# Linear attention into a gated feed-forward: the numerators of the first batches as pairs of 64-row products

## The chip, the cores and the metric

The kernel runs on one core of a Trainium2 chip. The metric is the device time of one execution in microseconds; a profile of one execution is read beside it. Engines: TensorE (PE, with its weight loads as PEld), VectorE (DVE), ScalarE (ACT), GpSimd (POOL) and SyncE (SP).

## The reference

Inputs q, k, v are 8 batches x 8 heads x 576 positions x 64; the feed-forward weights are 512 x 1536 (gate, value) and 1536 x 512 (out). Everything is float32 outside the kernel.

```python
def phi(x, c, s):
    r = np.maximum(x, 0.0)
    return np.concatenate([r * c, r * s], axis=-1)      # c, s: cos and sin of pi/2 * pos/S
q_p, k_p = phi(q, cos_w, sin_w), phi(k, cos_w, sin_w)
kv  = np.einsum('bhsf,bhsd->bhfd', k_p, v)
z   = np.sum(k_p, axis=2)
num = np.einsum('bhsf,bhfd->bhsd', q_p, kv)
den = np.einsum('bhsf,bhf->bhs', q_p, z)[..., None] + 1e-06
x   = (num / den), heads side by side                    # 4608 tokens x 512
g   = x @ w_gate
out = (g * (1.0 / (1.0 + np.exp(-g))) * (x @ w_val)) @ w_out
```

## The kernel before

**Tiles and groups.** A token tile `t` holds 128 tokens: two slots `c` of 64 positions. A batch has `NC` = 9 slots, so tile 4 holds the last slot of batch 0 and the first of batch 1. Four tiles make a token group `tg`, which goes through the feed-forward; nine groups. Groups 1 and up use a Strassen-like scheme for the products (`block_jobs`, L977, and `out_jobs`, L1142) beside plain ones (L904, L1052, L1262).

**Heads.** The 8 heads are numbered 2g + e, with e = 0 or 1 and g = 0 to 3; g is split again as 2j + i. Heads with i = 0 have their 64 features on SBUF rows 0 to 63, heads with i = 1 on rows 64 to 127.

**The attention numerators.** `kvd` (batch 0) and `kvd1` (batch 1) hold, for each e, j and w (w = 0 for cosine, 1 for sine), a block-diagonal matrix: the kv of the head i = 0 in the upper 64 rows and first 65 columns, the kv of the head i = 1 in the lower 64 rows and last 65 columns, zeros elsewhere. The 65th column of a head is z, so a product gives 64 numerators and the denominator. A product with 128 rows and 130 columns does two heads at once; the two w accumulate in PSUM. A tile takes 8 such products, and two PSUM banks hold its result. Batches 2 to 7 are done otherwise (L785: one head per product, cosine and sine on 128 rows, 65 columns) and aren't touched.

- Tiles 0 to 3, in a start phase written out by hand in `words`: `a_tile` (L372) makes the products, in two halves j = 0 and 1; `x_den` (L388), `x_rec` (L397) and `x_mul` (L401) divide, on VectorE; `x_turn_pe` (L418) turns x with the identity on TensorE; `x_turned` (L323) copies it to `xT`. For tile 0 the halves are separate down to the copies, and half j has PSUM bank j to itself; for tiles 1 to 3 bank e holds the heads of that e. `z` words put idle products (L187) between. `turn_q` (L351) turns the queries in between and `weight_q` (L360) makes the sine-weighted ones.
- Tiles 4 to 8: `tile_jobs` (L779 for batches 0 and 1) with the same block-diagonal products; tile 4's go in halves of 64 tokens, by batch. The denominators are on ScalarE (L797), reciprocal and multiplication on VectorE (L803, L807). Tiles 4 to 7 are turned on TensorE (L755); tile 8, like all later ones, by a transposing DMA (L747). `turned_tiles` (L1310, L1326) makes their queries.

**The order.** The words of the start phase are issued in the order written. The middle of them reads:

```
kvo10@dve a0.0 kvo11@act qr1@dve z1 den0.0 qw1.1
a0.1 den0.1 tq3 rec0.0 rec0.1 tq2 a1.0 a1.1 z2 x0.0 qr3@act x0.1 den1 xt0.1 qw3.1 xt0.0 rec1 qr2@act
xc0.1@act qw2.1 a3.0 x1.0 a3.1 a2.0 den3 xc0.0@act a2.1 G1.0 xt1.0
```

Everything later is a list of jobs with costs, due times and rooms (banks, buffers), which a planner in the kernel (`order_once`) puts into one order per engine while the program is built. The waits themselves come from the framework, which orders accesses to the same memory. The planner's costs for the touched jobs aren't changed, nor the number of jobs or their rooms.

## Time and profile before

| what | value |
|---|---|
| time, median of 3 runs | 298.6 us (298.52 to 299.35) |
| span of the profiled execution, first to last instruction | 296.4 us |
| mean granted TensorE clock | 0.998 |
| TensorE busy | 291.1 us, 98% |
| VectorE busy | 252.0 us, 85% |
| ScalarE busy | 199.4 us, 67% |

The profile is of one execution, for which only its span is given; the timed runs include what lies around the span, so the median stands 2.2 us above it. A line such as L779 is the line of the kernel that issued the instruction. Lengths of matmuls overlap, since they are pipelined: what one costs is read from start to start. A shape like 128\*64 128x130 is the weights (rows\*columns) and the moving operand (rows x columns).

### The profile page before, as it was taken

What the parts mean: (1) busy time and instruction counts of PE and PEld (TensorE: products, weight loads), DVE (VectorE), ACT (ScalarE), POOL (GpSimd) and SP (SyncE); (2) the same over time, 40 slices, a digit from 0 to 9 for tenths busy, and PEclk for the clock granted to TensorE, in tenths of its full rate; (3) what the DMA queues carried; (4) which work ended last, traced back from release to release, by engine and by line L of the source; (5) the groups of instructions that cost most, each with busy time, mean ns of one, the idle gap of its engine ahead of it and who ended that gap; (6) DMA issues with size and microseconds to landing.
All of it is one profiled execution on the core that took longest, in us unless ns stands there. A gap on an engine that the chain in (4) does not pass through costs nothing.

```text
span 296.4 us, 8073 instructions
## 1 busy us (share of the span) xinstructions
PE 291.1 (98%) x3244; PEld 238.7 (81%) x3244; DVE 252.0 (85%) x514; ACT 199.4 (67%) x421; POOL 69.6 (23%) x122
## 2 busy tenths in 40 slices
PE   8999999999999999999999999999999999999994
PEld 4597465776787888898898889888988888888883
DVE  7878997879877999999988987998679868986883
ACT  6564346989559968985699589967465556565630
POOL 7963630003007012221352023200220050002000
PEclk9999999999999999999999999999999999999999
DMA  7999999997989997799996979940470046002026
GB/s 266 225 196 198 202 206 207 203 205 121 194 177 144 229 190 122 151 171 149 174 203 133 186 113 162 183 81 2 107 110 2 0 97 119 2 0 73 0 58 157
DMA packets 71973, 40.89 MB, mean 138 GB/s; under 512 B 48768, under 2 KB 68736, under 8 KB 71936
## 3 DMA queue, kind: packets, MB, share of 16 engines
q0 software_dynamic: 24800, 24.39, 49.1%
q1 hardware_dynamic: 46528, 15.47, 28.9%
q10 hardware_dynamic: 608, 0.52, 0.7%
q8 instruction: 25, 0.41, 0.6%
q14 instruction: 12, 0.10, 0.1%
HBM read 37.75 MB, written 9.44 MB: 159 GB/s over the span
## 4 chain that ended last, share of the span: by engine, by line
PE 97%; DVE 1%; issue 0%
PE banks L977 45%; PE banks L1142 24%; PE banks L1052 5%; PE banks L1262 4%; PE banks L438 4%; PE banks L904 4%; PE banks L187 3%; PE banks L716 3%; PE banks L785 2%; PE banks L779 1%; PE banks L372 1%; PE banks L1310 0%; PE banks L315 0%; PE banks L418 0%; PE banks L351 0%
## 5 line engine op out<-in xcount | busy, mean ns | idle before, releaser
L1111 POOL DMA_DIRECT2D out_dram<-ob x52 | 27.3, 532 | 104.8 <-ACT ob L630 69.7
L1036 ACT ACTIVATE sg<-banks 128x512 bf16<-128x512 f32 x72 | 41.3, 599 | 5.6 <-PE banks L977 5.4
L977 PEld LDWEIGHTS <-wg_sb 128*128 128x128 f16 x384 | 36.9, 98 | 6.3
L628 ACT COPY banks<-banks 128x512 f32<-128x512 f32 (+1 forms) x53 | 29.9, 572 | 17.5 <-PE banks L977 7.3
L1142 PEld LDWEIGHTS <-ht 128*128 128x128 f16 x384 | 37.4, 98 | 4.8
L1072 DVE TENSOR_TENSOR ht<-sg,banks 128x512 f16<-128x512 bf16 x60 | 39.9, 680 | 0.9 <-PE banks L977 0.6
L977 PEld LDWEIGHTS <-wgs_sb 128*128 128x128 f16 x368 | 35.7, 98 | 4.6
L997 DVE TENSOR_TENSOR banks<-m,banks 128x512 f32<-128x512 f32 x44 | 30.2, 693 | 10.6 <-ACT m L628 8.1
L977 PEld LDWEIGHTS <-wv_sb 128*128 128x128 f16 x320 | 31.0, 98 | 3.8
L977 PE MATMUL banks<-kvt,wgs_sb 128*128 128x256 f16 x236 | 33.4, 273 | 0.0
L1142 PEld LDWEIGHTS <-sums 128*128 128x128 f16 x288 | 27.9, 98 | 3.3
L630 ACT ACTIVATE ob<-banks 128x512 f32<-128x512 f32 x32 | 18.8, 596 | 15.9 <-PE banks L1142 15.2
L977 PE MATMUL banks<-xT,wg_sb 128*128 128x256 f16 x192 | 28.8, 273 | 0.0
L628 ACT COPY m<-banks 128x512 f32<-128x512 f32 x44 | 25.5, 590 | 4.4 <-PE banks L977 4.3
L1142 PE MATMUL banks<-wo_sb,ht 128*128 128x256 f16 x192 | 25.7, 273 | 0.0
L1142 PE MATMUL banks<-wt_sb,sums 128*128 128x256 f16 x192 | 24.9, 273 | 0.0
L977 PE MATMUL banks<-xT,wv_sb 128*128 128x256 f16 x160 | 24.0, 273 | 0.0
L1036 ACT ACTIVATE sg<-m 128x512 bf16<-128x512 f32 x24 | 15.1, 630 | 12.4 <-DVE m L1005 12.2
L807 DVE TENSOR_TENSOR x<-banks,rec 128x512 f16<-128x512 f32 x32 | 21.6, 686 | 1.5 <-DVE rec L803 0.2
L977 PE MATMUL banks<-kvt,wg_sb 128*128 128x256 f16 x168 | 22.4, 273 | 0.0
L1142 PE MATMUL banks<-wt_sb,ht 128*128 128x256 f16 x192 | 22.3, 273 | 0.0
L877 ACT ACTIVATE r_q<-raw_q,tanq 128x256 bf16<-128x256 bf16 x45 | 20.7, 510 | 0.1
(160 smaller groups left out, 544.7 us busy)
## 6 DMA issues: line engine op xcount, KB each, us to landing
out_dram<-ob POOLq DMA_DIRECT2D x52, 128.0 KB, 3.9
raw_kv<-in_k_dram POOLq DMA_DIRECT2D x7, 576.0 KB, 5.9
raw_q<-in_q_dram POOLq DMA_DIRECT2D x12, 288.0 KB, 10.7
raw_kv<-in_v_dram POOLq DMA_DIRECT2D x6, 576.0 KB, 8.3
out_dram<-ob SPq DMA_DIRECT2D x12, 128.0 KB, 2.5
wg_sb<-in_moe_w_gate_dram POOLq DMA_DIRECT2D x5, 256.0 KB, 8.9
wv_sb<-in_moe_w_val_dram POOLq DMA_DIRECT2D x5, 256.0 KB, 9.5
wo_sb<-in_v_dram SPq DMA_DIRECT2D x2, 576.0 KB, 4.2
```

The costliest lines, as they stand in the source:

```text
L438: nc.tensor.matmul(out=st["f", tg, fc, lo][i], lhsT=(wg_sb, wv_sb)[i][:, kc, fs], rhs=xT[tg][:, ts, kc], start=(kc == 0), stop=(kc == KC - 1))
L628: nc.scalar.copy(out=out, in_=in_)
L630: nc.scalar.mul(out=out, in_=in_, mul=mul)
L807: tt(out=one(x_all, x).rearrange("p (y e d) -> p e y d", e=2, d=D), in0=view()[:, :, :, 0:D], in1=rec_all[:, t % 4].rearrange("p (e y) o - ...
L877: nc.scalar.activation(out=home()[:, :, c, 1], in_=raws[b, "q"][:, :, c], func=AF.Relu, scale=tanq[:, c:c + 1])
L977: nc.tensor.matmul(out=to[:, i], lhsT=a[:, c, 2 * u + i], rhs=x()[:, :, c], start=first and i == 0 and c == 0, stop=c == KH - 1, skip_grou ...
L997: tt(out=bank(c), in0=one(m7_all, m).rearrange("p i x -> p (i x)"), in1=bank(b), op=ALU.add)
L1036: nc.scalar.activation(out=gates(rooms[w])[:, :, jh * HT:(jh + 1) * HT], in_=src, func=AF.Silu, scale=DOWN)
L1052: nc.tensor.matmul(out=bank(v), lhsT=wv_sb[:, kc, fc * P:(fc + 1) * P], rhs=xT[tg][:, :, kc], start=(kc == 0), stop=(kc == KC - 1))
L1072: tt(out=ht[:, 4 * u + w:4 * u + w + 3:2, jh * HT:(jh + 1) * HT], in0=gates(rooms[w])[:, :, jh * HT:(jh + 1) * HT], in1=src.rearrange("p ( ...
L1111: {"POOL": nc.gpsimd, "SP": nc.sync, "ACT": nc.scalar}[j.eng].dma_start(out=out_v[idx // NC, idx % NC][:, cols], in_=ob_of(t)[e * SH:(e + ...
L1142: nc.tensor.matmul(out=to, lhsT=a[:, kc, i * P:(i + 1) * P], rhs=b[:, kc], start=first and kc == 0 and i == 0, stop=kc == HC - 1, skip_gro ...
```

## The change

Each product of 128 rows and 130 columns becomes two of 64 rows and 65 columns: one per head, on that head's rows only, without the zeros. The head i = 0 writes one PSUM bank, the head i = 1 the other, and the two are issued one after the other. So a tile takes 16 products instead of 8, with 16 weight loads; tile 4, in halves of 64 tokens, 32 instead of 16. This is so for tiles 0 to 8; tile 0 loses its separate banks for the halves. The result `x` then has its 128-column blocks in another order, which the turns on TensorE undo (`by_pairs`). Tile 8 is turned by a DMA, which can't, so its multiplication is split in two, one per j, that write the old order.

```diff
+    def by_pairs(kc):
+        return kc % 2 * J + kc // 2
+    def halves_of(i):
+        return slice(i * D, (i + 1) * D)
...
     def a_tile(t, j):
...
         for e in range(2):
             for w in range(2):
-                nc.tensor.matmul(
-                    out=(ps[:, j, 2 * e * D1:2 * (e + 1) * D1] if t == 0 else
-                         ps[:, e, 2 * j * D1:2 * (j + 1) * D1]),
-                    lhsT=(qwT[t % 2] if w else qr[t])[:, e, j].rearrange("p c s -> p (c s)"),
-                    rhs=kvd[:, e, j, w].rearrange("p i x -> p (i x)"),
-                    start=(w == 0), stop=(w == 1),
-                )
+                for i in range(2):
+                    rows = halves_of(i)
+                    nc.tensor.matmul(
+                        out=ps[:, i, (2 * j + e) * D1:(2 * j + e + 1) * D1],
+                        lhsT=(qwT[t % 2] if w else qr[t])[rows, e, j].rearrange("p c s -> p (c s)"),
+                        rhs=kvd[rows, e, j, w, i], start=(w == 0), stop=(w == 1))
...
     def x_den(t, ps, ys=slice(0, 4)):
...
-            in0=a_view(t, ps, ys)[:, :, :, D:D1],
+            out=heads(st["den", t])[:, :, ys], in0=by_rows(ps)[:, :, ys, D:D1],
...
     def x_turn_pe(t, ks=slice(0, KC)):
...
-            nc.tensor.transpose(out=ps[:, kc], in_=st["x", t][:, kc * P:(kc + 1) * P], identity=ident16)
+            nc.tensor.transpose(out=ps[:, kc], in_=st["x", t][:, by_pairs(kc) * P:(by_pairs(kc) + 1) * P], identity=ident16)
...
     def tile_jobs(t, key, by_pe=False):
...
                         if b < 2:
-                            if g % 2:
-                                continue
                             for w in range(2):
-                                nc.tensor.matmul(
-                                    out=ps[ms, e, g * D1:(g + 2) * D1],
-                                    lhsT=late[:, 2 * (t % 2) + w, e, g // 2].rearrange("p c s -> p (c s)")[:, ms],
-                                    rhs=(kvd1 if b else kvd)[:, e, g // 2, w].rearrange("p i x -> p (i x)"),
-                                    start=w == 0, stop=w == 1)
+                                for i in range(0 if g % 2 else 2):
+                                    rows = halves_of(i)
+                                    nc.tensor.matmul(
+                                        out=ps[ms, i, (g + e) * D1:(g + e + 1) * D1],
+                                        lhsT=late[rows, 2 * (t % 2) + w, e, g // 2].rearrange("p c s -> p (c s)")[:, ms],
+                                        rhs=(kvd1 if b else kvd)[rows, e, g // 2, w, i], start=w == 0, stop=w == 1)
                             continue
...
         def fn(j):
-            tt(out=one(x_all, x).rearrange("p (y e d) -> p e y d", e=2, d=D), in0=view()[:, :, :, 0:D],
-               in1=rec_all[:, t % 4].rearrange("p (e y) o -> p e y o", e=2).to_broadcast([P, 2, 4, D]), op=ALU.mult)
+            x_, rec_ = one(x_all, x), heads(rec_all[:, t % 4])
+            if pairs and not by_pe:
+                for jj in range(J):
+                    ys = slice(2 * jj, 2 * jj + 2)
+                    tt(out=x_.rearrange("p (j i e d) -> p j i e d", i=2, e=2, d=D)[:, jj], in0=view()[:, :, ys, 0:D],
+                       in1=rec_[:, :, ys].to_broadcast([P, 2, 2, D]), op=ALU.mult)
+                return
...
```

More of the change, by code (lines that the diff above doesn't have):

```diff
@@ L371, in a_tile, with by_rows, heads @@
             for w in range(2):
-                nc.tensor.matmul(
-                    out=(ps[:, j, 2 * e * D1:2 * (e + 1) * D1] if t == 0 else
-                         ps[:, e, 2 * j * D1:2 * (j + 1) * D1]),
-                    lhsT=(qwT[t % 2] if w else qr[t])[:, e, j].rearrange("p c s -> p (c s)"),
-                    rhs=kvd[:, e, j, w].rearrange("p i x -> p (i x)"),
-                    start=(w == 0), stop=(w == 1),
-                )
-    def a_view(t, ps, ys):
-        if t == 0:
-            return ps[:, ys.start // 2, 0:4 * D1].rearrange("p (e y x) -> p e y x", e=2, x=D1)
-        return ps[:, :, 0:2 * J * D1].rearrange("p e (y x) -> p e y x", x=D1)[:, :, ys]
+                for i in range(2):
[4 more added lines that the diff above has]
+                        rhs=kvd[rows, e, j, w, i], start=(w == 0), stop=(w == 1))
+    def by_rows(ps):
+        return ps[:, :, 0:2 * J * D1].rearrange("p i (y x) -> p i y x", x=D1)
+    def heads(ap):
+        return ap.rearrange("p (i y) o -> p i y o", i=2)
     def x_den(t, ps, ys=slice(0, 4)):
@@ L388, in x_den @@
         nc.vector.tensor_scalar(
-            out=st["den", t].rearrange("p (e y) o -> p e y o", e=2)[:, :, ys],
-            in0=a_view(t, ps, ys)[:, :, :, D:D1],
+            out=heads(st["den", t])[:, :, ys], in0=by_rows(ps)[:, :, ys, D:D1],
             scalar1=eps_all[:, 2 * t:2 * t + 1], scalar2=DOWN, op0=ALU.add, op1=ALU.mult)
@@ L396, in x_rec @@
             st["x", t] = x_all[:, t % NX]
-        nc.vector.reciprocal(out=st["rec", t].rearrange("p (e y) o -> p e y o", e=2)[:, :, ys],
-                             in_=st["den", t].rearrange("p (e y) o -> p e y o", e=2)[:, :, ys])
+        nc.vector.reciprocal(out=heads(st["rec", t])[:, :, ys], in_=heads(st["den", t])[:, :, ys])
     def x_mul(t, ps, ys=slice(0, 4)):
         nc.vector.tensor_tensor(
-            out=st["x", t].rearrange("p (y e d) -> p e y d", e=2, d=D)[:, :, ys],
-            in0=a_view(t, ps, ys)[:, :, :, 0:D],
-            in1=st["rec", t].rearrange("p (e y) o -> p e y o", e=2)[:, :, ys].to_broadcast(
-                [P, 2, ys.stop - ys.start, D]), op=ALU.mult)
+            out=st["x", t].rearrange("p (i y d) -> p i y d", i=2, d=D)[:, :, ys], in0=by_rows(ps)[:, :, ys, 0:D],
+            in1=heads(st["rec", t])[:, :, ys].to_broadcast([P, 2, ys.stop - ys.start, D]), op=ALU.mult)
     xT = {}
@@ L754, in fn @@
             for kc in range(KC):
-                nc.tensor.transpose(out=ps[:, kc], in_=one(x_all, x)[:, kc * P:(kc + 1) * P], identity=ident16)
+                nc.tensor.transpose(out=ps[:, kc], in_=one(x_all, x)[:, by_pairs(kc) * P:(by_pairs(kc) + 1) * P], identity=ident16)
         mm = pe(230, fn, key, after=after, get=[r], put=[x])
@@ L791, in view @@
         def view():
-            return bank(r)[:, :, 0:2 * J * D1].rearrange("p e (y x) -> p e y x", x=D1)
+            return by_rows(bank(r))
+        pairs = bs[-1] < 2
         def fn(j):
-            o, i_ = den_all[:, t % 4].rearrange("p (e y) o -> p e y o", e=2), view()[:, :, :, D:D1]
+            o, i_ = heads(den_all[:, t % 4]), view()[:, :, :, D:D1]
             if j.eng == "ACT":
@@ L806, in fn @@
         def fn(j):
-            tt(out=one(x_all, x).rearrange("p (y e d) -> p e y d", e=2, d=D), in0=view()[:, :, :, 0:D],
-               in1=rec_all[:, t % 4].rearrange("p (e y) o -> p e y o", e=2).to_broadcast([P, 2, 4, D]), op=ALU.mult)
+            x_, rec_ = one(x_all, x), heads(rec_all[:, t % 4])
[5 more added lines that the diff above has]
+                return
+            tt(out=x_.rearrange("p (i y d) -> p i y d" if pairs else "p (y e d) -> p e y d", d=D, **({"i": 2} if pairs else {"e": 2})),
+               in0=view()[:, :, :, 0:D], in1=rec_.to_broadcast([P, 2, 4, D]), op=ALU.mult)
         mul = Job({"DVE": d1(512)}, fn, after=[rec], get=[x], put=[r, one_at])
```

## The prediction

> **What bounds the kernel now.** I read the page first, then the busy time by stretches, then the timeline of TensorE (PE) where the change sits.

> ```profile
> span 296.4 us, 8073 instructions
> PE 291.1 (98%) x3244; PEld 238.7 (81%) x3244; DVE 252.0 (85%) x514; ACT 199.4 (67%) x421; POOL 69.6 (23%) x122
> PE 97%; DVE 1%; issue 0%
> ...
> 12.00:18.40 6.40, 6.39 (x107) 5.45 (x107) 5.65 (x20) 3.58 (x9) 5.15 (x7) 1.00 1.58 189
> ...
> 57.00:292.00 235.00, 234.87 (x2619) 203.15 (x2618) 203.40 (x386) 166.41 (x351) 42.51 (x78) 1.00 0.68 119
> ```

> The third line is the chain of work that ended last: 97% PE. The last two lines are the stretches (window, its length, then PE, PEld, DVE, ACT and POOL busy, granted clock, DMA). From 57 to 292 us PE is busy 234.87 of 235.00 us at full clock. So a nanosecond taken off PE's issue before that counts at the end, unless some input of PE is then late. Busy time isn't issue time, though; what PE's issue costs must be read from starts.

> ```profile
> 45.10 0.63 PE L779 MATMUL banks<-phit 128*128 128x130 bf16 x8
> 45.57 0.39 PE L755 MATMUL banks<-ident,x 128*128 128x128 f16 x4
> 45.79 0.63 PE L779 MATMUL banks<-phit 128*128 128x130 bf16 x8
> 46.26 0.59 PE L1262 MATMUL banks<-wo_sb,ht 128*128 128x512 f16 x2
> ...
> 65.81 0.42 PE L785 MATMUL banks<-kv,phit 128*128 128x65 bf16 x8
> 66.07 0.60 PE L977 MATMUL banks<-xT,wgs_sb 128*128 128x256 f16 x4
> ...
> 206.28 0.60 PE L977 MATMUL banks<-xT,wv_sb 128*128 128x256 f16 x4
> 206.81 0.46 PE L785 MATMUL banks<-kv,phit 128*64 128x65 bf16 x16
> 207.20 0.61 PE L1142 MATMUL banks<-wt_sb,ht 128*128 128x256 f16 x4
> ...
> L977 PE MATMUL banks<-xT,wg_sb 128*128 128x256 f16 x192 | 28.8, 273 | 0.0
> ```

> All but the last line are PE's timeline: start, length, line, tiles, weights, moving operand, count. The last is a group of the page; one product of 256 columns is 273 ns long. Three prices come from them:
> - An old product, 128 rows by 130 columns: (45.57 - 45.10)/8 = 0.059 us. One tile of eight takes 0.47 us.
> - A product of 65 columns on the whole array: (66.07 - 65.81)/8 = 0.0325 us, weight load included.
> - A tile of 16 products of 65 columns on half the array each (here halves by column), two at a time. Before it, four products of 256 columns at (0.60 - 0.27)/3 = 0.11 us would end their slots at 206.72; the half-array work starts at 206.81, so the **change of array shape costs 0.09 us** going in. From its start to the next shape's first product is 0.39 us: eight pairs at 0.0325 = 0.26, and 0.13 for coming out. In and out together: 0.48 us.

> Nothing in the trace of before does what the change does, half the rows with all 128 columns in pairs. The nearest on both counts:

> ```profile
> 38.37 1.24 PE L716 MATMUL banks<-phit,raw_kv 64*64 64x130 bf16 x72
> 39.59 0.38 PE L1262 MATMUL banks<-wo_sb,ht 128*128 128x512 f16 x1
> ...
> 8.03 0.22 PE L242 MATMUL banks<-wt_sb 64*128 64x128 f16 x1
> 8.18 0.61 PE L187 MATMUL banks<-zeros 128*128 128x512 bf16 x2
> ...
> 7.80 0.09 PEld L240 LDWEIGHTS <-wt_sb 64*128 64x128 f16 x1 [0.42 <-issue]
> 7.82 0.10 PEld L242 LDWEIGHTS <-wt_sb 64*128 64x128 f16 x1
> ```

> L716 runs 64x64 quarters: 72 products in 39.59 - 38.37 - 0.09 = 1.13 us are 0.016 each, a quarter of 0.059. So halves by row do run side by side, when they write different banks, as both there and in the change. L242 is a 64x128 product of 128 columns; its slot is 0.055 (four transposes of 128 columns fill 45.57 to 45.79), yet the next full-array product starts 0.15 later. So the 64x128 shape pays 0.09 too. The two weight loads of that shape start 0.02 apart, so two per pair fit into 0.0325 or nearly (0.03 to 0.04). I take 0.0325 per pair; upper end 0.065, if the two take turns; a lower end below 0.0325 has no row.

> [...]

> **The change, part by part.**

> *Tiles 4 and 5* (L779, now 64-row products).

> ```profile
> 41.41 0.24 PE L779 MATMUL banks<-kvt,phit 128*64 128x130 bf16 x1
> 41.41 0.24 PE L779 MATMUL banks<-phit 128*64 128x130 bf16 x1
> 41.49 0.22 PE L779 MATMUL banks<-kvt,phit 128*64 128x130 bf16 x1
> ...
> 41.84 0.80 PE L779 MATMUL banks<-phit 128*64 128x130 bf16 x9
> 42.57 0.64 PE L1310 MATMUL banks<-ident,raw_q 128*64 128x128 bf16 x16
> ```

> Tile 4 spans both batches, so its products already go by halves of the columns, in pairs (41.41 twice). From its first product to L1310, the next shape, the two tiles take 42.57 - 41.41 = 1.16 us, with three shape changes: in, between them, out. After the change there are three as well (128x128, 64x64, 64x128, 128x64). Tile 4 becomes 32 products in four streams of eight, tile 5 sixteen in two streams of eight: 0.26 + 0.13 each, 0.78 us together. **-0.38 us.** Ends: if rows don't overlap, 2 x (0.52 + 0.13) = 1.30, +0.14.

> *Tiles 6, 7, 8* stand alone between 128x128 work (45.10 to 45.57, 45.79 to 46.26; tile 8 likewise). Each goes from 0.47 to 0.09 + 0.39 = 0.48: what the pairs save, two new shape changes take. **+0.03 us** for the three.

> *Tile 8's multiplication* becomes two of half the size.

> ```profile
> 55.95 0.68 DVE L807 TENSOR_TENSOR x<-banks,rec 128x512 f16<-128x512 f32 x1
> ...
> 13.50 0.74 DVE L401 TENSOR_TENSOR x<-banks,rec 128x256 f16<-128x256 f32 x2
> ```

> Two halves take 0.74, one whole 0.68: +0.06 us on VectorE (DVE), which is 0.06 us for the sum that follows it there. Its result goes to a transposing DMA, for a token group that PE comes to later. I price it at 0, at most 0.06.

> *Tiles 0 to 3* (L372), the start.

> ```profile
> 12.24 0.41 PE L372 MATMUL banks<-kvt,wt_sb 128*128 128x130 bf16 x4
> 12.48 0.38 PE L187 MATMUL banks<-zeros 128*128 128x512 bf16 x1
> 12.70 0.39 PE L372 MATMUL banks<-kvt,wt_sb 128*128 128x130 bf16 x4
> 13.02 0.64 PE L351 MATMUL banks<-ident,raw_q 128*64 128x128 bf16 x16
> 13.59 0.64 PE L372 MATMUL banks<-kvt,wt_sb 128*128 128x130 bf16 x8
> ...
> 17.05 0.40 PE L418 MATMUL banks<-ident,x 128*128 128x128 f16 x4
> ...
> 12.69 0.22 DVE L388 TENSOR_SCALAR den<-banks,eps 128x4 f32<-128x4 f32 x1
> 13.15 0.22 DVE L388 TENSOR_SCALAR den<-banks,eps 128x4 f32<-128x4 f32 x1
> 14.34 0.23 DVE L388 TENSOR_SCALAR den<-banks,eps 128x8 f32<-128x8 f32 x1
> 14.48 0.41 DVE L360 TENSOR_TENSOR wt_sb<-wt_sb,tanT 128x512 bf16<-128x512 bf16 x1
> 16.30 0.69 DVE L401 TENSOR_TENSOR x<-banks,rec 128x512 f16<-128x512 f32 x1
> ...
> 14.95 1.04 PE banks L372 x15
> ```

> Here a wait is added. Tile 0's halves had a bank each; now both halves write both banks. The second half (PE, 12.70) comes in the program after the first half's denominators (DVE, 12.69 to 12.91), which read those banks. If accesses are ordered by bank, it waits for them; if by columns, it does not, and the price is nil. I take the wait. PE picks up 0.06 after DVE lets go (L360 ends at 14.89, the chain has PE's L372 at 14.95): start 12.97 in place of 12.70. Queued behind it on PE are L351's transposes, for which ScalarE's relu waits, and tile 1. Four pairs 0.13 and 0.13 out: L351 at 13.23, +0.21; tile 1 likewise at 13.80. On DVE the second denominators wait too: last pair at 13.07, some 0.2 for its result (L785's length, 0.42 less seven steps) and 0.06 to pick up, so 13.33, +0.18. DVE then runs on to 14.24 (13.50 + 0.74), where before it paused: the next denominators start at 14.34, 0.10 after that end, though a DVE row that waits for nothing starts some 0.09 before the previous one ends (14.48 against 14.34 + 0.23 = 14.57). That slack, 0.19, takes up the 0.18. These denominators need tile 1, whose results come at 13.80 + 7 x 0.0325 + 0.2 = 14.23, as before (13.59 + 0.64). From there DVE is where it was.

> PE gets to tiles 3 and 2 later (two new shape changes), does them in 16 pairs, 0.52 instead of 16 x 0.059 = 0.94, and comes to the first gate products some 0.1 early. It can't use it: the turn at 17.05 waits for DVE's 16.30 + 0.69 = 16.99, plus 0.06. **0 us** for the start; ends: -0.1, and +0.2 if DVE's slack isn't there.

> [...]

> **Sum:** -0.38 + 0.03 + 0 + 0 = -0.35 us. The profiled span goes from 296.4 to about 296.05. The median of the runs is 298.6, 2.2 above the span; I leave those 2.2 alone: **298.2 us**.

> **The rivals.**
> - *The rows take turns* (slower). Then a pair costs 0.065. For: a product of 64 rows still loads 128 columns of weights, so there are twice the loads, and no row shows two such loads side by side in different rows. Against: L716's quarters, and loads 0.02 apart. Price: tiles 6 to 8 (0.09 + 0.52 + 0.13 - 0.47) x 3 = +0.81; tiles 4 and 5 +0.14; at the start tile 0's second half lasts to 13.36, tile 1 begins 0.34 late and takes 0.26 us longer, its result comes at 13.93 + 0.49 + 0.2 = 14.62, the denominators at 14.68, +0.34 for DVE and so for 17.05. Together +1.3: **299.9 us**. It decides from 0.041 per pair: there 40 pair slots (8 in each of five tiles) eat what was gained. [...]
> - *The shape isn't charged* (faster). If a 64x128 product between 128x128 ones drains nothing, tiles 6 to 8 take 0.26 each, -0.63, and 4 and 5 lose one or two charges, -0.2: **297.4 us**. L242's 0.15 speaks against it.
> - *The gain is given back* (no change). PE, 0.35 us early from 42 us on, meets an input that isn't early, or DVE's slack at 14.3 fails. For: PE never waits now, so the trace doesn't tell by how much its inputs lead. Against: inputs of that stretch come from PE's own results by way of ScalarE and DVE, and move with it. **298.6 us.**

> **How the numbers follow.** Forecast 0.48, its own range 297.7 to 298.5; given back 0.18 (298.4 to 298.9); turns 0.24; not charged 0.10. About 0.3%, 0.9 us, is what a measurement of this kernel can tell from no change: below 297.7 is faster, above 299.5 slower. Faster: 0.10, and 0.03 from the forecast's edge: 0.13. Slower: 0.24 and 0.01 of the given back: 0.25. The rest, 0.62, is the same. The range leaves out the uncharged case and what is above the turns: 297.6 to 299.9.

> **What would show it.** Right: a timeline of tiles 6 to 8 with 16 products in about 0.48 us including both changes; tiles 4 and 5 in 0.78 up to L1310; tile 0's second half at 12.97; the turn still at 17.05; the last PE work 0.35 us sooner. Wrong: pairs starting 0.05 or more apart (turns); no 0.09 on either side (not charged); PE gaps after 42 us that are no shape change (given back); the turn at 17.2 or later (slack not there).

## The result: slower, and by more from run to run

The changed kernel takes 300.8 us (median of 20 runs, 297.88 to 306.71), the kernel before 298.93 (20 runs, 298.36 to 299.35); the ratio is 1.0053, 95% interval 1.003 to 1.0075. Here and below, medians, ranges and counts are of all runs, while the ratios leave out runs more than 1.5% above the fastest of their kernel: 3 of 20 here, 4 of 12 for the tiles-only kernel and for the kernel before with 96 more rows, 3 of 12 for the late one, and one each for the changed kernel with 144 more rows and the kernel before with 160. The forecast was 298.2. The profiled execution is the fastest of the twenty, 297.88 us: one page can't show what the other nineteen lost, so it is read for the mechanism, and the spread of the runs for the size. The page, the stretches and the timeline of PE, after the change:

```profile
span 296.1 us, 8234 instructions
PE 290.0 (98%) x3324; PEld 237.2 (80%) x3324; DVE 252.1 (85%) x515; ACT 199.3 (67%) x421; POOL 69.3 (23%) x122
PE 95%; DVE 2%; DMA 1%; issue 1%
```

```profile
12.00:18.40 6.40, 5.69 (x133) 4.74 (x132) 5.48 (x20) 3.27 (x8) 5.17 (x8) 1.00 1.59 191
57.00:292.00 235.00, 234.76 (x2619) 203.15 (x2616) 203.42 (x386) 166.03 (x350) 42.09 (x78) 1.00 0.68 119
```

```profile
12.19 0.39 PE L187 MATMUL banks<-zeros 128*128 128x512 bf16 x1
12.68 0.30 PE L380 MATMUL banks<-kvt,wt_sb 64*128 64x65 bf16 x8
12.91 0.58 PE L351 MATMUL banks<-ident,raw_q 128*64 128x128 bf16 x14
...
14.59 0.43 PE L380 MATMUL banks<-kvt,wt_sb 64*128 64x65 bf16 x16
15.63 0.42 PE L380 MATMUL banks<-kvt,wt_sb 64*128 64x65 bf16 x16 [0.61 <-issue]
...
41.46 0.22 PE L782 MATMUL banks<-kvt,phit 64*64 64x65 bf16 x2
42.19 0.25 PE L1321 MATMUL banks<-ident,raw_q 128*64 128x128 bf16 x2
...
45.23 0.40 PE L758 MATMUL banks<-ident,x 128*128 128x128 f16 x4
45.56 0.42 PE L782 MATMUL banks<-phit 64*128 64x65 bf16 x16
45.91 0.60 PE L1273 MATMUL banks<-wo_sb,ht 128*128 128x512 f16 x2
```

From 41 us on the forecast is seen: tiles 4 and 5 take 42.19 - 41.46 = 0.73 us. At the start something is new: PE was busy 6.39 of 6.40 us from 12 to 18.4, now 5.69. In front of tile 2's products it stands 0.61 us "<-issue": no semaphore, no data. The view of all that PE waited for puts it shortest; the first row of each kernel is the wait for the first zeros, which all have:

```profile
PE banks L187 <- DVE zeros L182: 1.0, 1, 1.0
PE banks L380 <- issue: 0.6, 1, 0.6
```

The kernel before has the first of these rows and nothing else. The experiments start from the second.

### The profile page after: what moved, and what is told of

It is laid out like the page before. It is cut to its first block, busy times and chain, and to the rows that moved or that the text cites. A ratio compares the mean times of both kernels' runs of the same rounds, so it can differ in the third digit from the quotient of the medians.

```text
span 296.1 us, 8234 instructions
## 1 busy us (share of the span) xinstructions
PE 290.0 (98%) x3324; PEld 237.2 (80%) x3324; DVE 252.1 (85%) x515; ACT 199.3 (67%) x421; POOL 69.3 (23%) x122
## 4 chain that ended last, share of the span: by engine, by line
PE 95%; DVE 2%; DMA 1%; issue 1%
PE banks L988 46%; PE banks L1153 25%; PE banks L1063 5%; PE banks L1273 4%; PE banks L441 4%; PE banks L915 4%; PE banks L719 3%; PE banks L787 3%; DMA wo_sb<-in_v_dram 1%; DVE v L293 1%; PE banks L782 1%; PE banks L1321 0%; PE banks L380 0%; PE banks L315 0%; PE banks L758 0%
## 5 line engine op out<-in xcount | busy, mean ns | idle before, releaser
L988 PE MATMUL banks<-xT,wg_sb 128*128 128x256 f16 x192 | 28.8, 273 | 0.0
L1047 ACT ACTIVATE sg<-m 128x512 bf16<-128x512 f32 x24 | 15.1, 630 | 12.4 <-DVE m L1016 12.2
L818 DVE TENSOR_TENSOR x<-banks,rec 128x512 f16<-128x512 f32 x31 | 21.0, 688 | 1.3
## 6 DMA issues: line engine op xcount, KB each, us to landing
raw_q<-in_q_dram POOLq DMA_DIRECT2D x12, 288.0 KB, 10.9
```

Of the source, the lines that this page charges most:

```text
L818: tt(out=x_.rearrange("p (i y d) -> p i y d" if pairs else "p (y e d) -> p e y d", d=D, **({"i": 2} if pairs else {"e": 2})), in0=view()[: ...
L988: nc.tensor.matmul(out=to[:, i], lhsT=a[:, c, 2 * u + i], rhs=x()[:, :, c], start=first and i == 0 and c == 0, stop=c == KH - 1, skip_grou ...
L1047: nc.scalar.activation(out=gates(rooms[w])[:, :, jh * HT:(jh + 1) * HT], in_=src, func=AF.Silu, scale=DOWN)
```

## The experiments

Every run was timed beside the kernel before, whose median was 298.68 to 298.93 each time.

**The changed kernel again, each half alone.** `e1_again` is unchanged; `e2_start_only` keeps the pairs of tiles 0 to 3 (`a_tile` and its divisions) with the old `tile_jobs`; `e3_tiles_only` the other way round.

> The changed kernel, unchanged, for its spread and a profile of an execution that isn't its fastest. Known: 297.9 to 306.7 us over 20 executions, the profiled one 297.9 with a span of 296.1, before 298.4 to 299.4. Theory A (the start): in a longer execution the extra microseconds stand as PE gaps between 12 and 38 us, where products wait for VectorE or for weights from DMA; the rest is as in the short one. Theory B (the pairs of tiles 4 to 8): the extra stands at or behind 41 us. Theory C (PE's instruction stream): the extra stands as gaps in which PE waits for no engine and no DMA of the program. Under each the median is 299.5 to 302.

> Only tiles 0 to 3 go by pairs; tiles 4 to 8 are as before. Theory A: spread and median as the changed kernel's (median 300 to 301, some executions above 302). Theory B: as before, 298.4 to 299.4. Theory C (instructions): 64 of the 160 added instructions are in it, so the spread may be less, but is not gone.

> Only tiles 4 to 8 go by pairs; tiles 0 to 3 are as before. Theory A: the spread is that of before (within 1 us) and the median is the forecast gain, 0.35 below before: 298.5. Theory B: spread and median as the changed kernel's. Theory C: 96 of the 160 added instructions, some spread.

| kernel | median, us | lowest to highest (12 runs) | ratio, 95% |
|---|---|---|---|
| again | 300.95 | 299.04 to 303.24 | 1.0073 (1.004 to 1.0105) |
| start only | 299.15 | 298.58 to 300.15 | 1.0007 (0.9984 to 1.003) |
| tiles only | 299.76 | 297.45 to 306.32 | 0.9978 (0.9936 to 1.0019) |

What PE waited for beside the zeros, again, start only and tiles only in turn:

```profile
PE banks L380 <- issue: 1.1, 1, 1.1
PE banks L988 <- DMA xT<-x: 0.5, 1, 0.5
```

```profile
PE banks L380 <- issue: 0.8, 1, 0.8
```

```profile
PE banks L998 <- DMA xT<-x: 1.6, 1, 1.6
```

By the ratios neither half alone is shown to be slower than the kernel before (both intervals hold 1); the whole is. There are two kinds of loss in the traces: the issue wait, in the changed kernel, its repeat and the start-only kernel, and waits for a transposing DMA (`xT`), at 74.8 us in one run and 144.3 in another.

The issue wait always stands at the same place of PE's stream. Counting PE's weight loads and products in order, each as one row, from 0, the row behind the gap is number 447 in all three. What ends it shows in the DMA view, in stretches of 1 us that begin with a packet of the instruction queue, at 13.29 us in the changed kernel and at 14.70 in the repeat:

```profile
q8 instruction: 1, 0.02, 6.1%
```

```profile
q8 instruction: 1, 0.02, 5.9%
```

and the end of the gap in the repeat in its timeline:

```profile
15.43 0.44 PE L380 MATMUL banks<-kvt,wt_sb 64*128 64x65 bf16 x16
16.97 0.42 PE L380 MATMUL banks<-kvt,wt_sb 64*128 64x65 bf16 x16 [1.10 <-issue]
```

A packet of 0.02 MB (16 KB) takes 5.9% of 16 engine-us, 0.95 us. PE goes on at 15.63 and 16.97, 1.3 to 1.4 us behind the packet's end each time. I read it as PE having run out of instructions. The kernel before has such a packet from 13.75 to 14.70 too, so by the same 1.35 us its instructions were usable by about 16.05 (an estimate); its row 447 is a feed-forward product (L438), reached only at 16.72. The pairs at the start bring 48 more rows ahead of that point and run through them faster, and row 447 is tile 2's first product, due at 14.86.

If rows come in blocks of 256, an instruction added anywhere moves every later boundary to another product. So the next kernels move boundaries without touching the attention, or touch it without moving them, by the number of idle products of zeros at the very start:

```diff
-    idle_products(12)
-    idle_products(40, 16)
-    idle_products(4)
+    idle_products(8)            # e4: 96 more rows in about the same time
+    idle_products(94, 16)
+    idle_products(2)
```

**The kernel before with 96 more rows, tiles only with 80 fewer, and two others.** In `e5_tiles_rows` the three calls are (8), (4), (4). `e6_tiles_hold` is the tiles-only kernel with two holds on POOL that read tile 9 and tile 19 (`xT[2][0:1, 1, ...]`, `xT[4][0:1, 3, ...]`) where they read tile 8 and batch 5's features. `e7_tiles_late` issues two products of zeros, 512 columns, ahead of tile 5's. The first kernel has 94 small products, as in the diff; the 98 in its expectation is a slip, for 94 give the 96 rows.

> The kernel before with its attention untouched; only the idle products of zeros at the very start are 98 small and 10 large ones where they were 40 small and 16 large, so that every later instruction of PE stands 96 rows further on in its stream, as the pairs put it, at the same start-up time. Theory F (PE ran out of fetched instructions in front of tile 2's products): PE's stream comes in pieces of 256 rows, and the piece that begins near its row 447 is late. That row is then the turning of q for tile 3 or the products of tile 0 or 1 (L351, L372, at about 13.1 us), and PE stands there 0.7 to 2 us with no semaphore to wait for; the median goes up by 0.3 to 1.5, to 299.2 to 300.4. If the spread of the changed kernel (297.9 to 306.7) also comes from where later pieces begin, the spread of this kernel is like that of the tiles-only kernel (297.5 to 306.3). Theory R (the pairs themselves, or the time at which PE comes to a product, make the waits): no gap at row 447, 298.9 as before, highest run under 300.

> Tiles 4 to 8 by pairs, tiles 0 to 3 as before, and 40 fewer idle products at the start, so that from tile 8 on the rows of PE stand within 16 of where the kernel before has them. Theory F for the spread (later pieces of the instruction stream begin at bad places): the spread goes, highest run under 300, median 298.3 to 298.6 (the 0.38 gained at tiles 4 and 5). Theory R (PE comes 0.38 us earlier to the transposes and races the bulk loads): the spread stays as in the tiles-only kernel, a third of the runs over 300, median 299 to 300.

> Tiles 4 to 8 by pairs, tiles 0 to 3 as before, and two holds of the bulk loads on POOL read another tile: batch 3's loads wait until tile 9's transpose has landed, not tile 8's, and batch 6's until tile 19's has, not the features' of batch 5. Nothing else moves. Theory R (tile 9's or tile 19's transposes are issued 0.1 to 1.7 us ahead of 2 to 4 bulk loads and, when the lead is small, land 6 to 7 us after their issue instead of 2.4 to 4): the stalls of PE at 74.8 us (0.71 in the repeat of the changed kernel) and at 144.3 us (1.77 in the tiles-only kernel) cannot occur; the highest run comes down under 301, the median to 298.3 to 298.6. Theory F: nothing changes, median 299.8, runs up to 306.

> Tiles 4 to 8 by pairs, tiles 0 to 3 as before, and two idle products of 512 columns in front of tile 5's products, 0.43 us, which gives back the 0.38 us that the pairs of tiles 4 and 5 gained. If PE's coming earlier is what makes the later waits for transposes (R): spread as before the change, median 298.8 to 299.1, highest under 301. If it is the pairs' rows in the stream (F) or tile 8's split division: the spread stays, median near 300, runs up to 306.

| kernel | median, us | lowest to highest | ratio, 95% |
|---|---|---|---|
| before, +96 rows | 300.98 | 298.34 to 305.31 (12) | 1.0042 (1.0015 to 1.007) |
| tiles only, -80 rows | 298.49 | 298.02 to 298.81 (12) | 0.9989 (0.9976 to 1.0002) |
| tiles only, holds | 305.09 | 303.17 to 306.81 (6) | 1.0201 (1.0161 to 1.0241) |
| tiles only, late | 301.29 | 298.93 to 307.01 (12) | 1.0052 (1.0026 to 1.0078) |

The first two speak for the rows. The attention of the kernel before, with nothing but more idle rows ahead of it, is as slow and as uneven as the changed kernel; the pairs of tiles 4 to 8 with the rows taken out elsewhere are even, in the narrowest spread of all. The first isn't purely that: in its profile, whose span is 2.8 us longer, 0.2 stands in the idle products, 0.7 is a wait for raw queries at the start, and 1.7 comes behind tile 5. PE's coming earlier doesn't look like the reason: the last kernel, with 0.43 us given back, is slower still. PE's waits in the first and the last:

```profile
PE banks L977 <- DMA xT<-x: 1.4, 1, 1.4
PE banks L187 <- DVE zeros L182: 1.0, 1, 1.0
PE banks L351 <- DMA raw_q<-in_q_dram: 0.7, 1, 0.7
```

```profile
PE banks L1002 <- DMA xT<-x: 1.6, 1, 1.6
```

The second has an issue wait of its own, in the middle of tile 5's products; its timeline, and the instruction packet in a stretch from 40.66 us:

```profile
41.93 0.48 PE L792 MATMUL banks<-phit 64*64 64x65 bf16 x13
42.88 0.26 PE L792 MATMUL banks<-phit 64*128 64x65 bf16 x5 [0.47 <-issue]
```

```profile
q8 instruction: 1, 0.02, 5.9%
```

The row behind this gap is number 958, a weight load: 511 rows behind 447, and between the two stands one semaphore instruction of PE (at 39.43 us), so 512 instructions, two blocks of 256. The packet ends at 41.61, 1.27 ahead of 42.88. The block before begins with row 703, which runs at 38.37 here; the 256 rows in between, among them 72 quarter products at 0.016 us each and tile 4's pairs, are through by 42.2. Its packet begins 40.66 - 38.37 = 2.3 us behind that row, and in the changed kernel the one of row 447 begins 13.29 - 10.37 = 2.9 us behind row 191. So a block seems to be asked for when the one before it begins. In the four profiles with a gap of 0.47 us or more it was usable 4.5 to 5.8 us after that (42.87 - 38.37 here; row 191 at 10.37 and row 447 at 15.63 in the changed kernel). It also says why the gap that I expected in the first kernel didn't come: there row 191 is an idle product, at 7.28 us, the packet began at 10.79, and row 447 ran at 14.4.

The holds (third kernel) were a failure: the two transposes landed 2.4 and 4.7 us after their issue, without a wait of PE, but batch 3's loads started 2.4 us later than in the tiles-only kernel and landed 4.0 to 4.6 later. PE then waited 3.6 us for a bank that ScalarE empties (L641). ScalarE itself stood 4.2 us ahead of that copy, until a DMA that turns features (`phit<-r_q`) had landed, at 91.63 us where it took until 86.61 in the tiles-only kernel. The wait, ScalarE's row, and the stretches around it (PEclk is the number behind POOL):

```profile
PE banks L729 <- ACT m L641: 3.6, 1, 3.6
```

```profile
91.73 0.91 ACT L898 ACTIVATE r_q<-raw_q,tanq 128x256 bf16<-128x256 bf16 x2 [4.20 <-DMA phit<-r_q]
```

```profile
89.40:93.10 3.70, 0.14 (x2) 0.10 (x1) 0.84 (x2) 1.37 (x4) 0.62 (x2) 1.00 0.03 8
93.20:95.10 1.90, 1.90 (x73) 1.71 (x73) 0.94 (x2) 1.90 (x5) 1.90 (x4) 0.59 0.39 25
95.10:97.00 1.90, 1.90 (x10) 1.32 (x9) 0.34 (x1) 1.47 (x4) 1.16 (x3) 0.51 1.15 193
97.00:99.00 2.00, 2.00 (x30) 1.69 (x29) 1.00 (x3) 1.30 (x5) 0.25 (x1) 1.00 1.21 207
```

This run tells nothing on the spread.

**The whole change, the tiles, and the kernel before, at chosen rows.** The idle calls are (8), (118, 16), (2); (12), (16, 16), (4); and (7), (127, 16), (2).

> The changed kernel whole, with 118 small and 10 large idle products at the start where it has 40 small and 16 large: 144 more rows ahead of the work, in about the same time. Theory F: PE's rows are fetched in pieces of 256 that begin at rows 447, 703, 959, ...; a piece is asked for when the piece before it begins and is there 3.0 to 4.6 us later. 144 rows more move the bad boundary from tile 2's products (14.8 us) to row 303 of the work (11.7 us, the rows 256 ahead of it run at 5.6 us), and put every boundary behind tile 8 at 48 rows from where the kernel before has it, among the shifts that ran without spread (0, 16, 64). So: no gap of PE in front of tile 2, 0.38 us won at tiles 4 and 5 and kept, median 298.2 to 298.5, highest run under 300. Theory R (pairs as such): median 300 to 301, runs to 306.

> Tiles 4 to 8 by pairs, tiles 0 to 3 as before, 24 fewer small idle products at the start: every boundary behind tile 8 stands 48 rows from that of the kernel before, and the boundary that stopped PE for 0.63 us inside tile 5's products in the run with 80 rows fewer now lies at the end of tile 4's, where the rows 256 ahead of it run 5 us earlier. Theory F: no such gap, no spread, 297.8 to 298.3, faster than the kernel before by about 0.4. If the gap stays: 298.5 as with 80 rows fewer. Theory R: 299.8, runs to 306.

> The kernel before, attention untouched, with 160 more rows of idle products at the start: behind tile 8 every boundary of the instruction stream stands where the changed kernel has it. Theory F: the spread of the changed kernel comes with it, median 300 to 301, runs up to 304 to 306, without a single pair. Theory R: 298.8, highest under 300.

| kernel | median, us | lowest to highest | ratio, 95% |
|---|---|---|---|
| changed, +144 rows | 299.74 | 298.41 to 306.14 (12) | 1.0025 (1.0003 to 1.0047) |
| tiles only, -48 rows | 298.77 | 297.77 to 300.76 (12) | 1.0002 (0.9981 to 1.0023) |
| before, +160 rows | 301.58 | 300.42 to 306.93 (9) | 1.0095 (1.006 to 1.0131) |

The last kernel has no pair, and behind tile 8 it has the changed kernel's boundaries; it is as slow as the changed kernel or slower (the intervals overlap). But not all of that comes from the rows' places. Its idle products, and those of the first kernel, take longer, which both expectations left out. The first product of the work, in the kernel before, the last kernel and the first:

```profile
7.80 0.39 PE L240 MATMUL banks<-wt_sb 64*128 64x512 f16 x1
```

```profile
9.13 0.39 PE L240 MATMUL banks<-wt_sb 64*128 64x512 f16 x1
```

```profile
9.15 0.39 PE L240 MATMUL banks<-wt_sb 64*128 64x512 f16 x1
```

So some 1.3 us of the last kernel's 2.7 is a late start (an estimate from one profile each; with the old calls that product starts at 7.3 to 8.4). From the turns behind tile 5 (L1310) to the last product, PE takes 251.09 us in it and 249.44 before: 1.65 lost behind tile 5, without a single pair. So a loss behind tile 8 doesn't need the pairs. Its profile waits 1.5 us at 76 us, for tile 9's transpose, which was issued 0.2 us behind the first bulk load of batch 3 and landed 7.1 us later (2.4 in the kernel before, issued 1.7 ahead of that load); the wait, and the transposes of that moment:

```profile
PE banks L977 <- DMA xT<-x: 1.5, 1, 1.5
```

```profile
DMA to landing us min/median/max: 7.1/7.1/7.1
```

The other two came out above what I expected, 298.2 to 298.5 and 297.8 to 298.3. The first started its work 1.35 us late, as said; without that its median would be 298.4. In it the wait at row 447 moved to the last turn of tile 1's queries and shrank but didn't go (the block before it began at 7.70 us, 6.2 earlier):

```profile
13.93 0.22 PE L351 MATMUL banks<-ident,raw_q 128*64 128x128 bf16 x1 [0.28 <-issue]
```

In the second there is no issue wait, as expected, but one of 1.0 us for VectorE at 155.4 us, where the kernel before has none:

```profile
PE banks L998 <- DVE banks L1018: 1.0, 1, 1.0
```

**Two tiles by pairs, rows kept.** Tiles 6 to 8 win nothing and add 48 rows. `e11_two_tiles` goes by pairs only for tiles 4 and 5 and has 24 fewer small idle products, so that PE's stream is as long as before, row for row from tile 5 on; `e12_two_tiles_rows48` leaves the idle products alone.

```diff
-        pairs = bs[-1] < 2
+        pairs = t < 6             # and the old products, in tile_jobs, for b < 2 and t > 5
...
-    idle_products(40, 16)
+    idle_products(16, 16)         # e11 alone
```

> Only tiles 4 and 5 by pairs, which are the two that gain (0.38 us; tiles 6 to 8 gained nothing), and 24 fewer small idle products at the start for the 48 rows that they add: from tile 5 on every piece of PE's instruction stream begins at the same product as in the kernel before. Theory F: no gap (the run with the same rows up to tile 5 had 0.9 and 2.0 us to spare at the boundaries 447 and 959), the 0.38 us is kept, no spread: median 298.3 to 298.6 where the kernel before has 298.7 to 298.9, highest under 300. Theory R: spread and 299 to 300.

> The same two tiles by pairs with the idle products left as they were, so that the pieces behind tile 5 begin 48 rows off. The boundary 959 lies at the first product of tile 4, as in the tiles-only kernel, no gap there. Theory F: the 0.38 us is won and, as in the other kernel that stood 48 rows off (298.8, 297.8 to 300.8, a wait of 1.2 us at 155 us), given back in part: median 298.5 to 298.9, wider than the kernel with the rows taken out. Theory R: the same as that kernel.

The first takes 298.47 us (297.88 to 299.41), ratio 0.9987 (0.9974 to 0.9999); the second 298.69 (298.25 to 301.46), ratio 1.0006 (0.9986 to 1.0026). The page of the first and its waits of PE:

```profile
span 296.1 us, 8073 instructions
PE 290.7 (98%) x3244; PEld 237.9 (80%) x3244; DVE 252.1 (85%) x514; ACT 199.6 (67%) x421; POOL 67.5 (23%) x122
```

```profile
PE banks L187 <- DVE zeros L182: 1.0, 1, 1.0
```

No wait but the first, and the start times of VectorE's instructions, compared one by one with the kernel before, stand 0.08 us early ahead of tile 4 and 0.45 behind tile 5, and stay there to the end: 0.37 won and kept. Its median is 0.26 us under that of the kernel before. The interval just leaves out 1, and it is one of a dozen intervals, so the gain rests on the trace more than on it.

All kernels by how far, modulo 256 rows, the boundaries behind tile 8 stand from where the kernel before has them; behind each median, how many of its runs took over 300 us:

| rows | without pairs | with pairs |
|---|---|---|
| 0 | before, 298.7 to 298.9 (6 of 127) | two tiles 298.47 (0 of 12) |
| 16 | | tiles only 298.49 (0 of 12) |
| 48 | | tiles only 298.77 (1 of 12), two tiles 298.69 (1 of 12), whole change 299.74 (5 of 12) |
| 64 | | start only 299.15 (1 of 12) |
| 96 to 100 | before 300.98 (8 of 12) | tiles only 299.76 (5 of 12), late 301.29 (9 of 12) |
| 160 | before 301.58 (9 of 9) | whole change 300.8 (15 of 20), again 300.95 (11 of 12) |

The medians go by the rows of this table far more than by its columns. So do the ratios, but for the tiles-only kernel (0.9978, its interval holds 1): 0.9987 and 0.9989 at 0 and 16 rows, 1.0002 to 1.0025 at 48, 1.0007 at 64, 1.0042 and 1.0052 at 96 to 100, 1.0053 to 1.0095 at 160. The profiles agree: of the six at 96 to 160 rows (the holds aside), five have a wait of 0.5 us or more for a transposing DMA, all but that of the changed kernel's fastest run; of the seven at 0 to 64 rows, none has one.

A rival is left: idle products and pairs also move PE in time against the loads. The profiles speak against it. At the first turn behind tile 5 (L1310, 42.57 us before), the five that wait later stand 0.45 us early to 1.34 late, and the others 0.63 early to 1.52 late: the same stretch.

## Why the prediction was wrong

- **Tiles 4 and 5, -0.38**: right in mechanism and size. 0.73 us where 0.78 was worked out, against 1.16 before; in the two-tile kernel 0.37 stayed won to the end.
- **Tiles 6, 7, 8, +0.03**: right, nothing won. Tile 7 with both shape changes lasts from 45.23 + 4 x 0.055 = 45.45 to 45.91, 0.46 us; the changes are seen, and pairs keep the pace of 0.03. So "the rows take turns" and "the shape isn't charged" are both out. Twice the loads don't hold the pairs up: a load of the pairs (L782) lasts 92 to 110 ns after the change, one of L785 96 to 114 ns before it, and still the pairs start 0.03 us apart and the products of L785 0.0325, loads included. So the loads overlap.
- **The bank wait at the start**: right, though no row of before shows it. Tile 0's first denominators end at 12.62, its second half starts at 12.68:

```profile
12.41 0.21 DVE L395 TENSOR_SCALAR den<-banks,eps 128x4 f32<-128x4 f32 x1
14.03 0.22 DVE L395 TENSOR_SCALAR den<-banks,eps 128x8 f32<-128x8 f32 x1
```

VectorE's slack took it up: tile 1's denominators came at 14.34 before and 14.03 now, in a run whose start was 0.28 early.
- **"0 us for the start"**, and with it the sum, is the step that failed. It let PE go "in 16 pairs" from tile 3 to tile 2 and on to the gate products, as if instructions were always there. The term left out is the number of rows: the 16 or 32 more per tile were priced by their run time alone, and their places in blocks of 256 at nothing. At the start the price is the wait that ends behind an instruction packet. From tile 0's first product (12.24 us before, 11.96 after) to the first gate product of 256 columns PE takes 6.16 us in the kernel before, 6.49 in the changed kernel, 6.99 in its repeat and 6.73 in the start-only kernel: 0.33 to 0.83 us, where at most 0.2 was forecast. With 144 rows more ahead, which move the boundary, it takes 6.27. Before and after:

```profile
18.40 1.91 PE L438 MATMUL banks<-xT,wg_sb 128*128 128x256 f16 x16
```

```profile
18.45 1.91 PE L441 MATMUL banks<-xT,wg_sb 128*128 128x256 f16 x16
```

- **The rest of the miss** comes behind tile 5, and there added idle rows, without a pair, are enough: 1.65 and 1.72 us in the profiles of the kernel before with 160 and 96 more rows. No profiled run of the changed kernel was slower than 300.11 us, so what its slowest runs lost is not seen directly.
- **The span** of 296.1 us, forecast as 296.05, is luck. That run came to its first product of the work (L240) at 7.50 us, where the kernel before came at 7.80, which hid the 0.33 lost at the start. And nearly every run's time stands 1.7 to 1.9 us above its own span (297.88 and 296.1 here), not the 2.2 of the sum: the profile of before was of a run some 0.4 us under the median.
- **"Given back"** named the right symptom, an input of PE that comes late, with the wrong cause. PE's being 0.35 us early isn't needed for it (the late kernel and the kernels before with more rows wait too); more rows ahead are enough (the kernel before with 96 or 160). That they act by where the blocks begin is argued, not shown.
- **What stays open** is the path from there to the late transposes. The tiles-only kernel, the late one and the kernel before with 96 rows wait at the same place, for tile 19's transpose, which lands 6.7 to 7.0 us after its issue; in the kernel before it took 4.3. In those three the features of batch 5, turned by a DMA just ahead, landed 10.4 to 10.9 us after their issue, and the bulk loads that hold on them were issued only 0.3 to 0.7 us behind tile 19's transpose. In the kernel before, the two-tile kernels and the tiles-only one with 80 rows fewer, the features took 12.2 to 12.5, and the loads came 1.5 to 1.8 behind. All seven have one instruction packet at that feature transpose: in the four it starts late in it, at 134.6 to 135.9 us, in the three that wait at its beginning, at 127.1 to 128.4. That the place of one packet of some 1 us turns this race is an argument from the traces, and a weak one: in the changed kernel's fastest run the features landed after 10.7 us too, and tile 19's transpose was in time. No run tried it by itself, and why 0 to 64 rows are even and 96 to 160 aren't is not shown.

## What to carry to other kernels

Where PE issues small products, count its instructions, not only their time. In the five profiles here with such a wait, 256 rows (128 products with their loads) were through before the next block was usable, 4.5 to 6.2 us after they began; the waits are marked "issue", four at row 447 and one 512 instructions behind it. If instructions come in blocks, a change of their number moves every later boundary, so time it against the old kernel with the same number of idle rows added, before judging the change itself, and see that these take no longer than the old ones. And look at the spread of the runs beside the median: here a shift of 96 rows or more showed as scatter (the holds aside), 4.2 to 8.9 us from the lowest run to the highest, against 1.5 and 0.8 in the kernels with pairs at 0 and 16 rows, and one profile catches little of it.

## What the hardware showed beside it

- PE stood for 0.3 to 1.1 us, with the wait marked "issue", in five of the thirteen profiles since the change, each time at row 447 or two blocks behind it. Two of the packets that ended these waits began 2.3 and 2.9 us behind the first row of the block before, as if only one block were fetched ahead (an estimate from these times).
- After a wait of 3.6 us the granted clock fell: 0.59 from 93.2 to 95.1 us and 0.51 to 97.0 (the rows of the kernel with the holds), which lost another 1.9 x 0.41 + 1.9 x 0.49 = 1.7 us.
